# The front of an ordered list of steps rewritten: gate sums and tail before the first weights, first weight conversion before the first scores

## The chip, the cores and the metric

The kernel runs on one core of a Trainium2 chip. The metric is the device time of one execution in microseconds (us); the time before is the median of three runs. A core has five engines that each work through their own instructions in order and meet only through semaphores: TensorE (PE, matrix products; PEld is its weight load), VectorE (DVE), ScalarE (ACT), GpSimd (POOL) and SyncE (SP), which here issues nearly all transfers between device memory and the core.

## What is computed

An mLSTM-like recurrence over 32 sequences (4 batches, 8 heads, 768 steps, head size 40), whose output, laid out as 3072 tokens of 320 values, goes through a two-layer network with a piecewise quadratic between the layers:

```python
for t in range(S):
    m_new = np.maximum(f_gate[:, :, t] + m, i_gate[:, :, t])
    f_stab = np.exp(f_gate[:, :, t] + m - m_new)
    i_stab = np.exp(i_gate[:, :, t] - m_new)
    C = f_stab * C + i_stab * outer(v_t, k_t)
    n = f_stab * n + i_stab * k_t
    y[:, :, t] = sigmoid(o_gate_t) * (C @ q_t) / np.maximum(np.abs(n @ q_t), 1.0)
h = x @ w_in            # x: y as 3072 x 320, w_in 320 x 2048
g = np.where(h >= 1, h, np.where(h <= -1, 0, (h + 1) ** 2 / 4))
return g @ w_out        # w_out 2048 x 320
```

## The kernel before

The 768 steps are cut into 6 chunks of 128; chunk c of batch b is block n = 4c + b, so blocks 0 to 3 are the first chunks of the four batches. Four blocks give one tile of 512 tokens for the network (six tiles), each worked through in 16 slices of 128 hidden values.

The order of the work is a list written out by hand, `STEPS`: a string of names such as `main.0`, each of which runs one step of the program or the next part of a step that pauses (`main.0` stands in the list six times, once for each of its parts). A wrapper (`InOrder`) holds every engine to the order in which its instructions come from that list. The list orders each engine; how engines meet is settled by what they read and write, and by which of the eight PSUM banks (`ps`, 128 x 512 fp32) a product gets. All products take their bank from this one pool, and a bank is given again once its last reader is through.

Nearly every instruction carries the line number of the wrapper (L189) in the profile, so tiles tell the steps apart. The steps that the change and the prediction speak of:

- `fi`, `fb`, `id`, `cs`, `W.i`, `qk.n`, `vv`, `v.n`, `og`, `A.n`: transfers in, issued on SP. `id` brings `ident` (an identity matrix and constants). `W.0` brings `wraw`, the first eighth of w_in; `W.1` the first eighth of w_out. `qk.n` is two transfers into `raw` (queries and keys of block n), `vv` and `v` bring values (and keys) into `ow` or `vk`, `og.0` the output gates of chunk 0 into `sig`.
- `sums.0`, `gtail.0`: small VectorE instructions on the gates of chunk 0 (`fi`, `m`, `ah`, `ac`, `ex`), with copies on GpSimd. `gex.0`: TensorE transposes `ex`, ScalarE takes the exponentials into `G`.
- `mask.b` and `add.b`: two banks of exponents for block b; `mask` puts in the causal mask (`late_t`, `idb`), `add` sums of the gates (`pick`, `less`, `ac`). `dec.b.0` and `dec.b.1`: ScalarE takes the exponentials of the two banks into `Abc` (or `A` for block 3), and so frees them.
- `score.n`: products of queries and keys (`raw`) into two banks, then, in two more parts, VectorE multiplies `Abc` by them.
- `main.n`: the product of `Abc` with the scaled values (`v1.n` on GpSimd), the division, the gate `sig`, a transposition of the result `y` and its split into `xh` and `xl`, the input of the network.
- `bmax`, `bsum`, `btail`, `exps`: the gates of chunks 1 to 4 at once; in its second part `bmax.0` moves `m_r` to `m_b` by four transfers on SP.
- `w.0`: the five parts of the conversion of `W.0`: `mg` and `win` on ScalarE, `win` on VectorE, `wh` on ScalarE, `wl` on VectorE.
- `sig.0`: ScalarE's sigmoid over the gates of chunk 0. It is another table of functions than the exponentials', so an ACT_TABLE_LOAD stands ahead of it and another behind it.
- `hot.k`: k products of zeros with nobody reading them.
- `mm.x`, `relu.x`, `max.x`, `out.x`: the network's slices.

The lines that the prediction leans on most:

```python
nc.scalar.activation(sig[c], sig[c], AF.Sigmoid)                       # sig
...
nc.scalar.activation(A[:, 4 * hh:4 * hh + 4, :], T[n]["Ap"][hh]..., AF.Exp)   # dec, chunk 0
...
up = psum_a()                                                          # main, a bank
for h in range(H):
    nc.tensor.matmul(up[:, h * D1:(h + 1) * D1], M[:, h, :], t["v1"][:, h, :], start=True, stop=True)
```

Of the kernel before, what the change touches and what calls it, by code (L numbers as in the profile page):

```python
# [45 lines left out]


STEPS = (
    "fi.0 mask.1 fb.0 W.0 vv.0 mask.0 hot.2 sums.0 mask.3 qk.1 add.1 hot.2 add.0 qk.2 w.0 w.0 bmax.0 id.0 dec.1.0 "
    "dec.1.1 dec.0.0 score.1 qk.3 gtail.0 hot.2 hot.2 bmax.0 gex.0 score.1 mask.2 qk.0 add.2 dec.2.0 dec.2.1 vv.2 "  # L50
    "add.3 v.4 dec.3.1 v1.1 dec.3.0 score.1 og.0 W.1 dec.0.1 score.2 main.1 score.0 bsum.0 bsum.0 bsum.0 w.0 "
    "score.3 score.2 score.2 one.0 score.0 v.1 score.0 v1.2 btail.0 w.0 v1.0 sig.0 main.1 btail.0 hot.4 btail.0 "
    "btail.0 w.0 v1.3 main.0 score.3 v.0 main.0 W.2 hot.2 exps.0 main.0 main.1 main.2 hot.2 hot.2 qn.5 A.4 score.3 "
    "v2.4 main.2 main.2 main.0 w.1 v2.1 qk.4 main.0 w.1 cs.0 main.3 main.1 main.2 main.0 W.3 v.5 carry.4 main.3 "
    "main.3 hot.2 v2.0 qn.4 main.1 decs.0 main.1 v.2 w.1 carry.1 main.3 A.5 A.6 main.2 w.2 carry.0 main.2 main.3 "
    "main.3 prep.4 carry.0 w.2 v1.4 prep.4 v2.5 score.4 w.2 prep.4 decs.0 W.4 carry.1 w.3 -- score.4 mm.0 relu.0 "
    "max.0 mm.1 w.2 main.4 w.2 relu.1 main.4 W.5 carry.5 W.6 carry.4 v2.2 w.3 w.3 main.5 main.5 prep.5 prep.5 "
    "score.4 carry.2 carry.2 max.1 mm.3 relu.3 prep.5 mm.2 w.4 carry.5 qk.5 prep.6 main.4 relu.2 main.4 v1.5 max.3 "
    "w.4 w.4 carry.5 prep.6 w.5 qk.6 og.1 max.2 out.0 out.1 out.2 w.5 w.5 w.4 w.4 score.5 so.1 score.5 score.5 A.7 "
    "W.7 score.6 w.6 carry.4 carry.4 v.6 w.6 prep.7 score.6 prep.6 mm.5 w.6 score.6 v1.6 qn.6 sig.1 main.5 main.4 "  # L60
    "main.4 so.2 relu.5 so.2 max.5 main.5 mm.4 relu.4 w.6 main.5 w.6 qn.7 w.7 w.7 prep.7 out.3 main.6 main.6 main.6 "
    "v2.6 carry.6 max.4 mm.6 carry.5 w.7 gh.5 gl.5 carry.6 gh.4 so.3 so.3 v.3 v2.3 carry.3 W.8 outh.4.2.3 carry.6 "
    "w.8 w.8 mm.7 outh.4.0.1 gl.4 main.6 outl.4 outh.5.2.3 A.8 relu.6 carry.3 main.7 A.9 qk.7 score.7 w.8 main.5 "
# [965 lines left out]
```

## Time and profile before

| what | us |
|---|---|
| median of three runs (465.94, 466.06, 479.42) | 466.06 |
| the profiled execution's own time | 465.84 |
| its span, from the first to the last instruction | 464.1 |
| TensorE busy in it | 456.0 (98%) |
| VectorE, ScalarE, GpSimd busy | 350.7, 327.5, 144.1 |

The profile is of one execution. Times in its rows count from the start of the span; 1.74 us of the execution's own time lie around the span. Products are pipelined, so a busy TensorE says that it had products in flight, and the distance from one product's start to the next's says how fast they went.

### The profile page before, as it was taken

Reading aid. Unit: us, or ns where it says so; the run is one execution under the profiler, and the core shown is the slowest. Engines: PE = TensorE matmul, PEld = TensorE weight load, DVE = VectorE, ACT = ScalarE, POOL = GpSimd, SP = SyncE. Lnnn points to the kernel's source line nnn. Section 1 sums busy time; section 2 is a strip of 40 time slices with the busy share of each in tenths; the row PEclk is TensorE's granted clock in tenths of the full one; section 3 lists DMA queues with packets and bytes.
Section 4 is the critical chain, followed back from the end, with each engine's and each line's share of the span. In section 5 each row is a group of like instructions: output and inputs, shape, how many; then the busy total and the mean of one; then the engine's idle time right before and its main releaser. Section 6 shows DMA issues by size and latency. Waiting matters only on the chain.

```text
span 464.1 us, 8795 instructions
## 1 busy us (share of the span) xinstructions
PE 456.0 (98%) x3333; PEld 408.5 (88%) x3336; DVE 350.7 (76%) x625; ACT 327.5 (71%) x593; POOL 144.1 (31%) x153
## 2 busy tenths in 40 slices
PE   6999999999999999999999999999999999999996
PEld 3888789998899999999988899989988898989986
DVE  5786789998979889878999988786775985443523
ACT  3679999998985586877777666766777734464651
POOL 2364233212543624423425643433213231000000
PEclk9999999999999999999999999999999999999999
DMA  6899959726445442564165437234616000010001
GB/s 215 291 283 352 296 175 347 220 67 166 147 115 148 118 132 91 171 177 124 48 177 161 118 89 203 63 78 155 159 57 160 1 1 0 2 42 16 1 0 57
DMA packets 23048, 60.60 MB, mean 131 GB/s; under 512 B 2599, under 2 KB 9535, under 8 KB 23007
## 3 DMA queue, kind: packets, MB, share of 16 engines
q1 hardware_dynamic: 22719, 59.81, 43.2%
q8 instruction: 26, 0.43, 0.4%
q10 hardware_dynamic: 288, 0.25, 0.2%
q14 instruction: 15, 0.12, 0.1%
HBM read 55.96 MB, written 4.01 MB: 129 GB/s over the span
## 4 chain that ended last, share of the span: by engine, by line
PE 87%; DVE 4%; ACT 3%; DMA 3%; issue 1%; SPq 1%; DVEq 0%
PE ps L189 87%; DMA qs<-in_qs 1%; DMA ident<-in_cst 1%; ACT r L189 1%; DVE stk L189 1%; SPq L189 1%; DVE hv L189 1%; DVE r L189 1%; DVE gl L189 0%; ACT Abc L189 0%; ACT raw L189 0%; ACT win L189 0%; ACT mg L189 0%; DVE win L189 0%; DVE xl L189 0%
## 5 line engine op out<-in xcount | busy, mean ns | idle before, releaser
L189 PE MATMUL ps<-oh,gh 128*128 128x320 f32 x368 | 112.3, 315 | 0.1
L189 PE MATMUL ps<-ow,gh 128*128 128x320 f32 x368 | 110.1, 309 | 0.0
L189 PE MATMUL ps<-xh,wh 128*128 128x512 f32 x288 | 100.6, 403 | 0.1
L189 PE MATMUL ps<-xh,wl 128*128 128x512 f32 x288 | 98.2, 395 | 0.0
L189 ACT ACTIVATE r<-ps,half 128x512 f32<-128x512 f32 x96 | 65.6, 683 | 44.5 <-PE ps L189 39.4
L189 DVE SCALAR_TENSOR_TENSOR r<-ps,r 128x512 f32<-128x512 f32 x96 | 64.7, 685 | 39.0 <-ACT r L189 38.7
L189 DVE TENSOR_TENSOR gl<-r,gh 128x512 fp32r<-128x512 f32 x92 | 69.9, 769 | 25.7 <-ACT gh L189 24.7
L189 ACT CAST gh<-r 128x512 fp32r<-128x512 f32 x92 | 56.2, 617 | 46.4 <-PE ps L189 21.6
L189 PEld LDWEIGHTS ps<-oh,gh 128*128 128x128 f32 x368 | 69.1, 188 | 1.9 <-issue 0.3
L189 PEld LDWEIGHTS ps<-ow,gh 128*128 128x128 f32 x368 | 69.2, 188 | 1.3
L189 PE MATMUL ps<-oh,gl 128*128 128x320 f32 x368 | 70.2, 311 | 0.0
L189 PEld LDWEIGHTS ps<-xh,wl 128*128 128x128 f32 x288 | 54.1, 188 | 12.8
L189 ACT ACTIVATE r<-r 128x512 f32<-128x512 f32 x96 | 60.7, 633 | 3.0
L189 PE MATMUL ps<-xl,wh 128*128 128x512 f32 x192 | 60.3, 395 | 0.0
L189 PEld LDWEIGHTS ps<-oh,gl 128*128 128x128 f32 x368 | 58.1, 188 | 1.1
L189 PEld LDWEIGHTS ps<-xh,wh 128*128 128x128 f32 x288 | 50.3, 188 | 7.8 <-DVE Abc L189 0.2
L189 ACT ACTIVATE Abc<-Abc,nA 128x128 f32<-128x128 f32 x160 | 50.4, 391 | 0.1
L189 POOL TENSOR_TENSOR v<-vk,G 128x328 f32<-128x328 f32 x36 | 28.9, 807 | 53.2 <-DMA vk<-in_vk 28.2
L189 POOL TENSOR_TENSOR y<-y,z 128x320 f32<-128x320 f32 x24 | 21.1, 882 | 76.2 <-DVE y L189 76.2
L189 PEld LDWEIGHTS ps<-xl,wh 128*128 128x128 f32 x192 | 36.0, 188 | 8.8
L189 POOL TENSOR_TENSOR m<-m 128x1024 bf16<-128x1024 f32 x16 | 31.6, 1976 | 37.6 <-DVE m L189 35.0
L189 DVE SCALAR_TENSOR_TENSOR stk<-raw,ident,qs 120x1024 fp32r<-120x1024 f32 x28 | 37.9, 1356 | 2.9 <-ACT raw L189 2.8
(143 smaller groups left out, 665.4 us busy)
## 6 DMA issues: line engine op xcount, KB each, us to landing
qs<-in_qs SPq DMA_DIRECT2D x28, 480.0 KB
Abc<-a_d SPq DMA_DIRECT2D x20, 512.0 KB
vk<-in_vk SPq DMA_DIRECT2D x20, 324.0 KB
wraw<-in_w_in SPq DMA_DIRECT2D x8, 768.0 KB
wraw<-in_w_out SPq DMA_DIRECT2D x8, 640.0 KB
sig<-in_og SPq DMA_DIRECT2D x6, 640.0 KB
qn<-in_qn SPq DMA_DIRECT2D x20, 180.0 KB
raw<-in_qk SPq DMA_DIRECT2D x20, 160.0 KB
```

Source lines behind the costliest of these rows:

```text
L189: r = getattr(self.engine, name)(*args, **kwargs)
```

## The change

Only the string `STEPS` changes, and only its first 204 of 1621 words. The words are the same ones, each as often as before; from word 205 on (`mm.5`) the two lists are equal. The first lines of it:

```diff
-    "fi.0 mask.1 fb.0 W.0 vv.0 mask.0 hot.2 sums.0 mask.3 qk.1 add.1 hot.2 add.0 qk.2 w.0 w.0 bmax.0 id.0 dec.1.0 "
+    "fi.0 mask.1 fb.0 id.0 sums.0 gtail.0 W.0 mask.0 add.1 dec.1.0 dec.1.1 add.0 hot.2 hot.2 gex.0 w.0 w.0 bmax.0 "
```

What the list makes of each engine's order shows in the built programs. First SP's queue, the transfers behind the first three. Before (a number behind a name tells tiles of one name apart):

```order
L189 DMA wraw_139<-in_w_in 128x1536
L189 DMA ow_141<-in_vk 128x2x328
L189 DMA raw_174<-in_qk 40x2x512 x2
L189 DMA raw2_200<-in_qk 40x2x512 x2
L189 DMA ident_92<-in_cst 128x154
L189 DMA raw3_224<-in_qk 40x2x512 x2
L189 DMA m_b_239<-m_r_207 32x129 x4
L189 DMA raw_253<-in_qk 40x2x512 x2
L189 DMA ow_268<-in_vk 128x2x328
L189 DMA vk_280<-in_vk 128x648
L189 DMA sig_286<-in_og 128x1280
```

The same stretch of SP's queue with the changed list:

```order
L189 DMA ident_92<-in_cst 128x154
L189 DMA wraw_163<-in_w_in 128x1536
L189 DMA raw_231<-in_qk 40x2x512 x2
L189 DMA ow_234<-in_vk 128x2x328
L189 DMA raw2_251<-in_qk 40x2x512 x2
L189 DMA m_b_256<-m_r_205 32x129 x4
L189 DMA raw_265<-in_qk 40x2x512 x2
L189 DMA sig_279<-in_og 128x1280
L189 DMA ow_281<-in_vk 128x2x328
L189 DMA wraw_283<-in_w_out 128x1280
L189 DMA raw3_285<-in_qk 40x2x512 x2
```

`ident` is now ahead of the first weights, and the gates `sig` are ahead of the second pair of values (`ow`), of the values `vk` and of block 3's `raw3`.

Second, ScalarE from the first exponentials to the sigmoid. Here `Abc_143` is block 0 (banks 144 and 145), `Abc_130` block 1, `Abc_248` block 2 (banks 249 and 250), `A3` block 3. Before:

```order
L189 ACTIVATE Abc_143<-ps_144 128x512
L189 ACTIVATE G_117<-ps_244 128x128
L189 ACTIVATE Abc_248<-ps_249 128x512
L189 ACTIVATE Abc_248<-ps_250 128x512
L189 ACTIVATE A3_169<-ps_171 128x512
L189 ACTIVATE A3_169<-ps_170 128x512
L189 ACTIVATE Abc_143<-ps_145 128x512
L189 CAST wh_125<-win_205 128x3x256
L189 ACT_TABLE_LOAD
L189 ACTIVATE sig_286<-sig_286 128x1280
L189 ACT_TABLE_LOAD
```

ScalarE with the changed list, where `Abc_165` is block 0 and `Abc_226` block 2 (banks 227 and 228):

```order
L189 ACTIVATE win_203<-wraw_163 128x768
L189 ACTIVATE A3_210<-ps_212 128x512
L189 ACTIVATE A3_210<-ps_211 128x512
L189 CAST wh_125<-win_203 128x3x256
L189 ACTIVATE Abc_226<-ps_227 128x512
L189 ACTIVATE Abc_165<-ps_166 128x512
L189 ACTIVATE Abc_165<-ps_167 128x512
L189 ACT_TABLE_LOAD
L189 ACTIVATE sig_279<-sig_279 128x1280
L189 ACT_TABLE_LOAD
L189 ACTIVATE Abc_226<-ps_228 128x512
```

The last exponential of block 2 (`dec.2.1`, from bank 228) stood ahead of the sigmoid and now stands behind it and its two table loads.

Third, TensorE at `main.0`, behind its products of zeros, with what each row waits for. Before:

```order
L189 LDWEIGHTS zeros_90
L189 MATMUL ps_356<-zeros_90 128x512
L189 MATMUL ps_367<-ow_141,Abc_143 128x41 [waits DVE_49,Pool_49]
L189 MATMUL ps_367<-ow_141,Abc_143 128x41 x3
L189 MATMUL ps_367<-ow_141,Abc_143 128x41 [waits DVE_49]
L189 MATMUL ps_367<-ow_141,Abc_143 128x41 x3
```

The same place on TensorE with the changed list:

```order
L189 LDWEIGHTS zeros_90
L189 MATMUL ps_338<-zeros_90 128x512
L189 MATMUL ps_348<-ow_234,Abc_165 128x41 [waits DVE_49,Activation_49,Pool_49]
L189 MATMUL ps_348<-ow_234,Abc_165 128x41 x3
L189 MATMUL ps_348<-ow_234,Abc_165 128x41 [waits DVE_49]
L189 MATMUL ps_348<-ow_234,Abc_165 128x41 x3
```

The first product of `main.0` waited for VectorE and GpSimd and now waits for ScalarE too (Activation_49). In the built program it is a wait for ScalarE's thirteenth signal, which is given by `Abc_226<-ps_228`, the row behind the sigmoid; the bank of `main.0` (348) is the one that row reads.

## Rows read from the trace of the kernel before

**Rows 1.** The page's busy times: engine, busy us, share of the span, instructions.

```profile
PE 456.0 (98%) x3333; PEld 408.5 (88%) x3336; DVE 350.7 (76%) x625; ACT 327.5 (71%) x593; POOL 144.1 (31%) x153
```

**Rows 2.** The chain that ended last, in order of time: start, us, what.

```profile
12.07 7.82 PE ps L189 x88
...
302.27 158.24 PE ps L189 x1078
```

**Rows 3.** Busy us of each engine in two stretches; last, clock, DMA share, GB/s.

```profile
15.00:20.00 5.00, 4.95 (x63) 4.47 (x62) 4.76 (x12) 3.31 (x5) 2.61 (x3) 1.00 0.93 310
...
5.00:20.00 15.00, 13.17 (x132) 9.72 (x133) 10.30 (x26) 8.18 (x13) 4.86 (x8) 1.00 0.79 259
```

**Rows 4.** The timeline, TensorE to 7 us: start, us, engine, line, operation, tiles, count.

```profile
2.18 0.58 PE L186 MATMUL ps<-late_t,idb 128*128 128x512 bf16 x1 [2.18 <-POOL rst L186]
...
3.84 1.06 PE L189 MATMUL ps<-zeros 128*128 128x512 bf16 x2
...
5.59 0.39 PE L189 MATMUL ps<-ac,pick 96*128 96x128 bf16 x4
...
6.47 0.59 PE L189 MATMUL ps<-zeros 128*128 128x512 bf16 x2
...
6.91 0.39 PE L189 MATMUL ps<-ac,pick 96*128 96x128 bf16 x4
```

**Rows 5.** The timeline, TensorE from the gates' transposition to the third scores.

```profile
12.07 0.30 PE L189 MATMUL ps<-ident,ex 128*128 128x128 f32 x1 [0.23 <-DMA ident<-in_cst]
...
14.51 1.16 PE L189 MATMUL ps<-raw 40*128 40x128 f32 x16
...
15.60 1.98 PE L189 MATMUL ps<-ow,Abc 128*128 128x41 f32 x16
...
17.51 2.06 PE L189 MATMUL ps<-raw 40*128 40x128 f32 x32
```

**Rows 6.** The timeline, ScalarE; in brackets the idle time before, and its end.

```profile
6.95 0.90 ACT L186 ACTIVATE mg<-wraw 128x768 f32<-128x768 f32 x1 [4.93 <-DMA wraw<-in_w_in]
...
8.53 1.55 ACT L189 ACTIVATE Abc<-ps 128x512 f32<-128x512 f32 x3
...
14.62 1.09 ACT L189 ACTIVATE A<-ps 128x512 f32<-128x512 f32 x2 [0.24 <-PE ps L189]
...
17.43 0.83 ACT L189 CAST wh<-win 128x768 fp32r<-128x768 f32 x1 [1.25 <-DVE win L189]
...
21.25 1.27 ACT L189 ACTIVATE sig<-sig 128x1280 f32<-128x1280 f32 x1 [1.68 <-DMA sig<-in_og]
...
22.54 1.28 ACT L189 ACT_TABLE_LOAD   x1
...
23.83 0.66 ACT L189 ACTIVATE G<-ps 128x384 f32<-128x384 f32 x2
```

**Rows 7.** The timeline, VectorE: the scan of bmax.0, then gtail.0 and a copy.

```profile
6.68 1.27 DVE L189 TENSOR_TENSOR_SCAN m_r<-fi_r,m_r 32x512 f32<-32x512 f32 x1
...
7.99 0.28 DVE L189 TENSOR_TENSOR fi<-fi,m 32x128 f32<-32x128 f32 x1
...
9.19 0.14 DVE L189 COPY carry<-m_r 32x1 f32<-32x1 f32 x1
```

**Rows 8.** The timeline, SP's issues of m_b and of the gates sig.

```profile
7.98 3.37 SPq L189 DMA_DIRECT2D m_b<-m_r  x4
...
14.25 0.42 SPq L189 DMA_DIRECT2D sig<-in_og  x1
```

**Rows 9.** The transfers issued in the first 25 us: tiles, count, KB each.

```profile
raw<-in_qk SPq DMA_DIRECT2D x10, 160.0 KB
...
ow<-in_vk SPq DMA_DIRECT2D x2, 328.0 KB
...
vk<-in_vk SPq DMA_DIRECT2D x1, 324.0 KB
```

**Rows 10.** Busy us of each engine in the tail; then clock, DMA share, GB/s.

```profile
462.70:463.50 0.80, 0.00 (x0) 0.00 (x0) 0.00 (x0) 0.00 (x0) 0.00 (x0) 0.53 0.00 0
```

22 rows, old and new, of the table STEPS are left out of this document.

## The prediction

> **What bounds the kernel now.** I read the page's busy times first: TensorE is busy for 456.0 of 464.1 us [rows 1], so the span is TensorE's work plus some 8 us of waiting. The chain of waits says where those are: from 12.07 on it is TensorE's own products, with short detours, up to the last stretch, which ends at 302.27 + 158.24 = 460.51 [rows 2]. Then the stretches: between 15 and 20 us, in the middle of the part that is rewritten, TensorE is busy 4.95 of 5.00 us, while in the whole of 5 to 20 us it is busy 13.17 of 15 [rows 3]. So behind 12.07 nothing is waited for in the front, and what was waited before it, from 5 us on, is at most some 1.8 us. The list is a permutation: the products are the same, the products of zeros (`hot`) among them. Hence the rule for the sum: **the change costs or gives what it does to TensorE's idle time and to its rate in the front, and nothing else**. That ScalarE or VectorE do something earlier counts only where TensorE waits for it.
>
> **What the change removes.** The wait at 12.07 for `ident` [rows 5] goes: `ident` is fourth on SP's queue. Gate sums and tail run one behind the other on VectorE, ahead of the scan of `bmax.0`; that scan began at 6.68 and the tail took from 7.99 to 9.19, 1.20 us [rows 7]. So `ex` is ready 1.3 us earlier, and the scan and with it the `m_b` transfers, issued from 7.98 [rows 8], come 1.2 us later, at about 9.2. They stand ahead of `qk.0` and `og` on SP, so this holds back both; what they bring, `bsum` waits for, off TensorE's path until `exps`.
>
> **TensorE up to `main.0`.** Four mask products now run from 2.18 to some 3.9, where the products of zeros and `mask.3` followed before, and then TensorE waits for `ac` until 5.59 as it did [rows 4]. In the rows the products up to 3.84 start 0.42 us apart for 512 columns, which is 1.2 GHz, and at 6.47 two take 0.44, which is 2.4 GHz, though the clock column says 1.00 for all of it; TensorE had worked without a gap since 2.18 before the rate rose. With a gap of 1.7 us in that stretch the rise may come later. At the full rate `add.1` and `add.0` take 2 x 0.88 (5.59 to 6.47) and two pairs of zeros 2 x 0.44: the transposition of `ex` comes at 8.2. At half rate for as long as at the start (2.18 to 5.59, 3.4 us) 1.7 us are lost: 9.9. I take 9.9 and keep 8.2 for the range.
>
> From there to `main.0` TensorE has: transposition, one mask and two `add` 2.44 (12.07 to 14.51), `score.1`, `score.2`, `score.0` 1.09 each (14.51 to 15.60) [rows 5], another mask 0.44, and six pairs of zeros 2.62 [rows 4]: together 8.8. TensorE is ready for `main.0` at 17.0 to 18.7.
>
> **When `main.0` may start.** Its first product waits for `dec.2.1`, and that stands behind `sig.0` and two table loads. ScalarE, from the transposition at 9.9: `G` 0.34 later (12.07 to 12.41 is what it waited, and its row in the same stretch is 0.3 long), so free at about 10.5; `mg` and `win` 1.58 (6.95 to 8.53); two `A` 0.97; then `wh`, which waits for VectorE's `win` until about 13.1, 0.85; three `Abc` 1.45 to 1.55; one table load 1.28 [rows 6]: about 16.8. But `sig` also needs its gates. They landed at 21.25, where ScalarE had waited 1.68 us for them [rows 6], and were issued at 14.25 [rows 8]. With the new list 328 KB of `ow`, 324 KB of `vk` and 2 x 160 KB of `raw` (block 3) no longer stand ahead of them [rows 9]; at the 259 GB/s of 5 to 20 us [rows 3] these 972 KB are 3.75 us: 17.5. They can't be issued before about 12.1 to 13.2 (9.2, plus the four `m_b` in at most the 3.37 us of the row, plus `qk.0`), and 768 KB of `wraw`, nearly alone on the queues, took some 4.4 us from issue to `mg` at 6.95 [rows 6], so not before 16.0. I take 17.4, between 16.0 and 18.3.
>
> From the start of `sig` to the first work behind the second load the trace has 23.83 - 21.25 = 2.58; `dec.2.1` itself takes 0.6 [rows 6]. So `main.0` starts at 17.4 + 2.6 + 0.6 = **20.6**, and TensorE stands for 2 to 3.5 us.
>
> The Trainium skill, ScalarE: Activation LUTs, section What ACT_TABLE_LOAD costs, puts a switch at 2.66 us, 1.28 of load and 1.38 of drain. The load agrees with its row, but the next instruction starts at 23.83, 0.01 us behind the load [rows 6]: the trace shows no drain. By the page `main.0` would start 2.8 us later still; the row decides.
>
> **What that is worth.** Where would `main.0` have to start for the time to stay? Before, TensorE never waited from 12.07 on. Of the work that it did then, the new list has done ahead of `main.0`: 2.44 (transposition, mask, two `add`), two scores 2.18, and four of the pairs of zeros 1.75; the fifth score and the rest come behind it in both. Sum 6.4, less 0.1 for the two short gaps in these rows: 12.07 + 6.3 = **18.4** is break-even. So 20.6 - 18.4 = **+2.2 us**. Nothing behind can take it back, since TensorE did not wait there; nothing adds, if the order behind `main.0` keeps it fed: the `y` of `main.0` and `score.2` come through VectorE while TensorE has `main.1` (1.9 us, 15.60 to 17.51 [rows 5]) and a pair of zeros (0.44) to do, a cover of 2.3 us for the division on VectorE and one product on GpSimd. If that cover fails at one place, I allow 0.5, an estimate of one more VectorE instruction in the way. `w.0` done 4 us earlier is worth nothing: no product waited for it before, `mm.0` stands behind all four `main`.
>
> VectorE also does `wl` and two parts of `bsum` ahead of the products with `score.0`; `main.0` needs these products too. The wait for `dec.2.1` hides that; without it they would be next, and cost what they come after 18.7, when TensorE is ready.
>
> The sum is made against the profiled execution, 465.84, whose span is 464.1; it is 0.22 below the median. 465.84 + 2.2 = 468.0; on the median 466.06 + 2.2 = **468.3**.
>
> **The rivals.**
> 1. *The wait is as short as break-even, so not slower.* For this `sig` must begin by 18.4 - 3.2 = 15.2, so the gates must land within 3.1 us of the earliest issue and ScalarE be through its first load by then. The second can be, if the rate rises as early as before (16.8 less 1.7); the first has only the free queues for it, against 4.4 us of `wraw`. It would give 465.3 to 466.6. I give it 0.10; with what the change spares at 12.07 it reaches a gain of 0.5 at best.
> 2. *The clock falls while TensorE waits ahead of `main.0`, so slower still.* At the end of the trace TensorE's last product ended at 460.51 [rows 2], and from 462.70 to 463.50 the granted clock reads 0.53 [rows 10], about 1.2 GHz. So it had fallen some 2.2 us after the last product, and the wait that I expect is 2 to 3.5 us. From about 2.2 us on it decides: `main.0`, `main.1` and what follows run at half rate for a stretch like the one at the start, 3.4 us, and lose 1.7: 470.0. For it: the length. Against: one case, in the tail, where TensorE had nothing left. 0.25. The Trainium skill, TensorE: Matmul & The Clock Gate, section What's actually happening, also has the throttled clock as the idle state; no row here shows a wait of this length in the middle of the work.
>
> **The numbers.** Forecast 0.63, the clock 0.25, no slower 0.10, something else 0.02. The forecast's own bounds are the landing at 16.0 (where ScalarE's 16.8 takes over: `main.0` at 20.0, +1.6; with the early rise +1.2) and at 18.3 (+3.1, and 0.5 for a failed cover): 467.2 to 469.7. The range goes down to 466.5, which takes in a part of rival 1, and up to 470.7 for rival 2: outside is about 0.15. Two per cent, what a measurement tells from no change, are 9.3 us; no case comes near it, so faster 0.01, same 0.97, slower 0.02.
>
> **What would show it.** In the changed kernel's profile: `G` for chunk 0 near 10.3 and not 12.41; `wh` before 15 and not at 17.43; `sig` starting on a landing near 17.4; a wait of TensorE of 2 to 3.5 us that ends between 20 and 21.5 with ScalarE's `Abc` as its releaser, ahead of products from `ow` and `Abc`; no other wait of TensorE over 0.3 us behind it, and from `mm.5` on the same distances as before. I am wrong if that wait is under 1 us, if the gates land before 15.5, or if TensorE waits again further down for `xh`, `Abc` or weights.

## The result and the profile after

The changed kernel takes **470.48 us** (median of 4 executions, 470.39 to 470.60) against 466.09 for the kernel before on the same chip: a ratio of 1.0096, 95% interval 1.0079 to 1.0114. It is slower by 4.4 us where 2.2 were forecast. The profiled execution has a span of 468.7 us, 4.6 more than before. In some executions of several kernels here, the kernel before among them, the mean granted clock is only 0.97 to 0.98 and the time 473.5 us or more; the ratios leave most of those out, while the medians and ranges of single kernels include them.

The page's first lines of the changed kernel, span and busy time of each engine:

```profile
span 468.7 us, 8791 instructions
...
PE 459.4 (98%) x3333; PEld 410.4 (88%) x3336; DVE 352.1 (75%) x625; ACT 327.6 (70%) x593; POOL 142.4 (30%) x153
```

The same 3333 products are busy for 459.4 us, not 456.0 [rows 1]. So only 1.2 of the 4.6 us are idle time (9.3 instead of 8.1); **3.4 us are products that ran slower**. For that the forecast's sum had no term behind `main.0`.

TensorE's timeline, changed kernel (start us, us, what, count, in brackets the idle time ahead and what ended it):

```profile
5.65 0.58 PE L189 MATMUL ps<-ac,pick 96*128 96x128 bf16 x4 [1.60 <-DVE ac L189]
...
9.02 1.59 PE L189 MATMUL ps<-zeros 128*128 128x512 bf16 x4
10.44 0.27 PE L189 MATMUL ps<-ident,ex 128*128 128x128 f32 x1
...
15.58 1.90 PE L189 MATMUL ps<-zeros 128*128 128x512 bf16 x7
17.41 1.16 PE L189 MATMUL ps<-raw 40*128 40x128 f32 x16
18.50 1.04 PE L189 MATMUL ps<-zeros 128*128 128x512 bf16 x4
20.75 4.25 PE L189 MATMUL ps<-ow,Abc 128*128 128x41 f32 x32 [1.21 <-ACT Abc L189]
24.79 0.63 PE L189 MATMUL ps<-zeros 128*128 128x512 bf16 x1
25.64 0.42 PE L189 MATMUL ps<-ident,fi_b 128*128 128x128 f32 x1 [0.22 <-issue]
...
26.50 0.84 PE L189 MATMUL ps<-ident,y 128*128 128x128 f32 x3
...
28.36 0.55 PE L189 MATMUL ps<-ident,y 128*128 128x128 f32 x3
```

Read the same product in two places. Four products with `ac` lasted 0.39 at 5.59 before [rows 4]; at 5.65 they now last 0.58, and four zeros take from 9.02 to 10.44, 1.42 us, where two took 0.44 at 6.47 before [rows 4], so four 0.88. So TensorE is at 1.2 GHz up to some 10 us. Three transpositions of `y` last 0.84 at 26.50 and 0.55 at 28.36: it is at 1.2 GHz a second time. The windows of the changed kernel around that (last columns: granted clock, DMA share, GB/s) say from when to when:

```profile
20.75:23.80 3.05, 3.05 (x28) 3.05 (x28) 1.24 (x7) 0.00 (x0) 0.02 (x1) 1.00 1.06 307
23.80:27.21 3.41, 3.19 (x15) 2.66 (x15) 2.83 (x8) 0.47 (x2) 2.58 (x4) 0.50 0.98 348
27.21:30.00 2.79, 2.79 (x32) 2.61 (x32) 1.49 (x4) 2.67 (x8) 1.66 (x3) 1.00 1.00 350
```

From 23.80 to 27.21 the granted clock is 0.50. TensorE had 3.19 us of work there, half of which, 1.6 us, is the price. Of the rest of the 3.4, some 1.5 us belong to the first 10 us, which the forecast did see: TensorE worked about 6.3 us at the half rate there (2.19 to 4.05 and 5.65 to some 10.1), 3.4 before. Until it fell, TensorE had stood ahead of 20.75 and then run 28 of the 32 products of 128x41 in `main.0` and `main.1` without a gap.

ScalarE in the changed kernel, from `G` to the signal on which `main.0` waits:

```profile
10.75 0.28 ACT L189 ACTIVATE G<-ps 128x128 f32<-128x128 f32 x1 [2.60 <-PE ps L189]
...
13.69 0.83 ACT L189 CAST wh<-win 128x768 fp32r<-128x768 f32 x1
14.43 1.56 ACT L189 ACTIVATE Abc<-ps 128x512 f32<-128x512 f32 x3
16.01 1.28 ACT L189 ACT_TABLE_LOAD   x1
17.47 1.27 ACT L189 ACTIVATE sig<-sig 128x1280 f32<-128x1280 f32 x1 [0.17 <-DMA sig<-in_og]
18.75 1.28 ACT L189 ACT_TABLE_LOAD   x1
20.05 0.60 ACT L189 ACTIVATE Abc<-ps 128x512 f32<-128x512 f32 x1
```

From the landing of the gates on, this chain went as forecast, to within 0.15 us. The gates were issued at 12.74 and took 4.70 us (before 14.25 and 7.0).

### The profile page after: what moved, and what is told of

The parts are those of the page before. It is cut to its first block, busy times and chain, and to the rows that moved or that the text cites. A ratio compares the mean times of both kernels' runs of the same rounds, so it can differ in the third digit from the quotient of the medians.

```text
span 468.7 us, 8791 instructions
## 1 busy us (share of the span) xinstructions
PE 459.4 (98%) x3333; PEld 410.4 (88%) x3336; DVE 352.1 (75%) x625; ACT 327.6 (70%) x593; POOL 142.4 (30%) x153
## 4 chain that ended last, share of the span: by engine, by line
PE 95%; DMA 1%; DVE 1%; ACT 1%; SPq 1%; issue 0%; DVEq 0%
PE ps L189 95%; DMA sig<-in_og 1%; SPq L189 1%; DMA fi<-in_fi 0%; DVE m_r L189 0%; DVE fi L189 0%; ACT L189 0%; ACT sig L189 0%; DVE ac L189 0%; DVE ah L189 0%; DVE m L189 0%; ACT Abc L189 0%; ACT r L189 0%; DVE carry L189 0%; DVE less L186 0%
## 5 line engine op out<-in xcount | busy, mean ns | idle before, releaser
L189 DVE TENSOR_TENSOR gl<-r,gh 128x512 fp32r<-128x512 f32 x92 | 72.0, 791 | 25.3 <-ACT gh L189 24.3
```

The costliest lines, as they stand in the source:

```text
L189: r = getattr(self.engine, name)(*args, **kwargs)
```

## The experiments

Three theories were tried. **W** (in the first three expectations simply the theory): the standstill ahead of `main.0` lets the clock fall. **A** or **Z**: rows of thin products (`main`, 128x41) with no zeros among them do it, a standstill at most adding to them. **B**: the loss is only the half rate of the first 10 us. "The clock fell" below means a window at 0.50 behind the first rise; in an execution without one the mean clock reads 0.999 or 1.0, with one short stretch 0.996. By that measure it fell in the kernel before too, in 12 of 50 executions (in seven of them to 0.995 or 0.996, at 467.3 to 468.1 us). The diffs show only the words around each change of the list; the rest of a line is left out.

**1. `dec.2.1` ahead of `sig.0`** in the changed kernel.

```diff
-main.0 main.1 main.0 A.4 sig.0 main.0 hot.2 dec.2.1 btail.0
+main.0 main.1 main.0 A.4 dec.2.1 sig.0 main.0 hot.2 btail.0
```

> The changed kernel with dec.2.1 ahead of sig.0 in the list, so that the bank which main.0 takes over is read out before ScalarE turns to the gates; nothing else is moved. Theory (TensorE's wait for dec.2.1 puts main.0 at 20.75 instead of the break-even 18.4, and the half-rate stretch from 23.80 to 27.21 follows from that wait): main.0 starts near 19.4, where the last product of zeros ends and VectorE's score is done; no wait, the clock stays at 1.00; 470.5 - 1.4 - 1.7 = 467.4 us. Rival A (the clock falls because 32 thin products, 128x41, follow one another, wait or no wait): it falls some 3 us behind main.0's start, near 22.4; 470.5 - 1.4 = 469.1. Rival B (the loss is the half rate in the first 10 us, the wait only covers other waits): within 0.3 of 470.5.

468.28 us (467.68 to 471.47, 11 executions), ratio to before 1.0043 (1.0029 to 1.0057): half of the loss is gone. In eight of the eleven the clock read 0.999 or 1.0; in the profiled one, the longest, it fell twice, the first time although TensorE had not waited for anything since 5.5 us. Its timeline and windows:

```profile
18.00 1.04 PE L189 MATMUL ps<-zeros 128*128 128x512 bf16 x4
19.01 3.74 PE L189 MATMUL ps<-ow,Abc 128*128 128x41 f32 x32
22.57 0.39 PE L189 MATMUL ps<-zeros 128*128 128x512 bf16 x1
```

```profile
19.01:22.93 3.92, 3.92 (x34) 3.80 (x35) 3.31 (x12) 0.94 (x1) 0.89 (x2) 1.00 1.06 317
22.93:26.34 3.41, 3.29 (x22) 2.94 (x23) 1.94 (x6) 2.16 (x6) 3.09 (x5) 0.50 0.98 344
...
29.76:36.58 6.82, 6.60 (x32) 6.38 (x33) 3.49 (x12) 1.96 (x4) 4.93 (x6) 0.50 1.05 295
```

TensorE was busy for all of the 3.92 us ahead of the fall, so it need not stand for that; without the wait the fall is rarer, though (three of eleven; four of four in the changed kernel), and about as frequent as in the kernel before (12 of 50). The median lies between W (467.4) and A (469.1): the eight are nearer to W, while the profiled one shows that the fall does not need the wait. B is out.

**2. Zeros in the wait**, changed kernel.

```diff
-score.0 hot.4 A.6 btail.0 btail.0 main.0
+score.0 hot.10 A.6 btail.0 btail.0 main.0
```

> The changed kernel with hot.10 in place of hot.4 ahead of main.0: six products of zeros more, 6 x 0.217 = 1.3 us at the full rate, in the 1.4 us in which TensorE stood. They add work that the reference does not need. main.0 should start at 20.75 as in the changed kernel. Theory (the standstill lets the clock fall): the clock stays at 1.00 and the 1.7 us of the half-rate stretch go: 468.8. Rival A (the thin products make it fall): the stretch is still there, 470.5. Rival B (early half rate): 470.5 as well.

471.13 us (470.33 to 471.19, 4 executions). By its time this is A or B; its profile says otherwise:

```profile
19.56 2.33 PE L189 MATMUL ps<-zeros 128*128 128x512 bf16 x10
21.73 3.66 PE L189 MATMUL ps<-ow,Abc 128*128 128x41 f32 x32
```

```profile
21.73:25.66 3.93, 3.88 (x34) 3.74 (x34) 2.24 (x10) 0.00 (x0) 0.97 (x2) 1.00 1.03 306
25.66:32.87 7.21, 7.17 (x68) 6.69 (x68) 6.82 (x20) 3.15 (x8) 4.63 (x7) 1.00 0.87 310
32.87:36.28 3.41, 3.19 (x16) 3.24 (x16) 1.68 (x5) 2.09 (x5) 3.20 (x5) 0.50 1.05 287
```

With zeros right ahead, the same 32 products left the clock at 1.00. But `main.0` came 1 us later, since the clock's first rise came late in this execution and the zeros themselves had to be run, and the clock fell at 32.87, behind the next thin row (`main.2`, `main.3`). The expectation overlooked that row, and the gain at the first place was lost at the second. In all four executions the mean clock reads 0.996 or less, so here the clock fell each time with no wait ahead of the products.

**3. The wait kept, zeros between `main.0` and `main.1`**, changed kernel.

```diff
-main.0 main.1 main.0 A.4 sig.0 main.0 hot.2 dec.2.1
+main.0 hot.2 main.1 main.0 A.4 sig.0 main.0 dec.2.1
```

> The changed kernel with the pair of zeros hot.2, which follows main.1's products, put between those of main.0 and of main.1: the same products, the wait ahead of main.0 as it is, but the row of 32 thin products is cut into 16 and 16. Theory (the standstill decides): the clock falls near 23.8 as before, 470.5 within 0.4. Rival A (the long row of thin products decides): no fall, 468.8. Rival B: 470.5.

470.59 us (470.36 to 477.98): no change, as W said. In the profiled execution, the longest, the clock fell at 23.08, after a standstill of 1.63, `main.0` (20.73 to 22.51) and the two zeros. The other three read 0.996 as well. So 16 thin products behind a standstill are as bad as the 32.

**4. Zeros in the early gap**, changed kernel.

```diff
-W.0 mask.0 add.1
+W.0 mask.0 hot.4 add.1
```

> The changed kernel with hot.4 behind mask.0: four products of zeros more in the 1.6 us in which TensorE waits for ac near 4 us; they add work that the reference does not need. The clock should rise near 5.4 as in the kernel before, and the transposition of ex come at 8.7 instead of 10.44. Theory (the gates' landing at 17.4 and ScalarE behind it set main.0): main.0 still starts within 0.3 of 20.75, TensorE only waits some 3 us ahead of it; 470.2 to 471.5 with the fall of the clock. Rival B (the half rate of the first 10 us is what is lost): main.0 1.7 us earlier and 468.8.

478.78 us, the lowest 471.91: the time itself is not to be compared. Its profile answers the question, though:

```profile
9.31 0.27 PE L189 MATMUL ps<-ident,ex 128*128 128x128 f32 x1
...
17.37 1.04 PE L189 MATMUL ps<-zeros 128*128 128x512 bf16 x4
20.61 6.18 PE L189 MATMUL ps<-ow,Abc 128*128 128x41 f32 x32 [2.20 <-ACT Abc L189]
```

TensorE was 1.1 us earlier at `ex` and at the last zeros, and `main.0` stayed where it was: behind ScalarE. What the first 10 us lose is covered in the changed kernel, and B is out. In it TensorE stood 1 us longer, and the clock fell already at 21.53 and stayed down until 45.42; only one of the four executions came below 477 us.

**5. `dec.2.1` ahead of `sig.0`, and zeros moved into the early gap.**

```diff
-W.0 mask.0 add.1 dec.1.0 dec.1.1 add.0 hot.2 hot.2 gex.0
+W.0 mask.0 hot.2 hot.2 add.1 dec.1.0 dec.1.1 add.0 gex.0
```

> The run with dec.2.1 ahead of sig.0, and the two pairs of zeros that follow add.0 moved ahead of add.1, into TensorE's wait for ac: the same products as the changed kernel. Its measure is the run without this move, 468.28, and 467.7 in the executions whose clock did not fall. With zeros in that gap the clock rose at 7.88 instead of 9.28 to 10.14. Reason (early half rate and gap are paid as soon as ScalarE no longer sets main.0): ex is transposed near 8.5, main.0 starts 1.0 to 1.5 us earlier, near 17.5 to 18, no wait over 0.3 ahead of it; 466.2 to 466.9, so level with the kernel before (466.0). Rival (VectorE's score, behind wl and bsum, sets main.0 as well): it starts near 18.7 and no more than 0.3 us are gained: 467.5 or above. The thin products of main.0 and main.1 still stand in one row of 32, so that the clock may fall as in the run before, + 1.7 and more in such an execution.

467.70 us (465.78 to 471.78, 10 executions), ratio 1.0042 (1.0013 to 1.0071). `main.0` started at 17.97 in the profiled execution, 1.0 earlier than in experiment 1, and the shortest executions, 465.78, 466.08 and 466.34, are level with before, as expected: once ScalarE is out of the way, the early gap is paid. The median is higher, mainly because the clock fell in five of the ten (mean clock 0.989 to 0.996), in the profiled one at 27.20, in the products of `main.3`. Two executions whose clock did not fall took 467.18 and 468.09 all the same; why is not known, since they were not profiled.

**6. The same, with two pairs of zeros moved among the thin products.**

```diff
-v.1 score.2 hot.2 hot.2 v.0 bsum.0 cs.0 hot.2 dec.0.0
+v.1 score.2 hot.2 v.0 bsum.0 cs.0 dec.0.0
...
-main.0 main.1 main.0
+main.0 hot.2 main.1 main.0
...
-main.2 main.2 main.2 main.3 decs.0
+main.2 main.2 main.2 hot.2 main.3 decs.0
```

> The run before this one (dec.2.1 ahead of sig.0, zeros in the early gap) with two pairs of zeros taken out of the row of seven near 15 us and put between the products of main.0 and main.1 and between those of main.2 and main.3: no product more than in the changed kernel. Theory Z (the clock falls where thin products, 41 columns each, follow one another for long with no 512-column products among them, a standstill counting like them): no fall in the front in any execution, 466.3, and the executions within 1 us of one another. Theory W (the standstill decides): this run has none either, so no fall, and the run without the spread has none as well: the two within 0.3 of each other.

472.76 us (467.27 to 479.06, 9 executions), ratio 1.0104 (1.0059 to 1.0148): worse, and neither theory said so. The clock fell in seven of the nine. In the profiled execution, the longest, the place that the zeros were taken from suggests why:

```profile
13.12 1.04 PE L189 MATMUL ps<-zeros 128*128 128x512 bf16 x3
14.95 0.46 PE L189 MATMUL ps<-raw 40*128 40x128 f32 x2 [0.79 <-DMA raw<-in_qk]
15.87 1.13 PE L189 MATMUL ps<-raw 40*128 40x128 f32 x14 [0.47 <-DMA raw<-in_qk]
16.93 1.71 PE L189 MATMUL ps<-zeros 128*128 128x512 bf16 x4
18.44 3.48 PE L189 MATMUL ps<-ow,Abc 128*128 128x41 f32 x16
```

The row of seven had covered the first of these waits for `raw` (experiment 5 has only the second, 0.47). Now TensorE stood 0.79 and 0.47 us there, and the clock fell at 17.14, ahead of `main.0`, whose 16 products took 3.3 us instead of 1.7.

**7. The kernel before, its zeros moved out of the thin rows**, with no new wait for ScalarE.

```diff
-dec.0.1 score.2 main.1 score.0
+dec.0.1 score.2 hot.2 hot.2 hot.2 main.1 score.0
...
-main.0 W.2 hot.2 exps.0 main.0 main.1 main.2 hot.2 hot.2 qn.5
+main.0 W.2 exps.0 main.0 main.1 main.2 qn.5
```

> The kernel before the change, with three pairs of zeros (the one behind main.0's products, the two behind main.2's) moved ahead of main.1's products: the same products, no new wait for ScalarE, and none among the thin products from main.0 to the first zeros behind main.3, some 7 us. Theory Z (the row of thin products lets the clock fall): the granted clock falls to 0.5 between 22 and 30 us though TensorE never stands: 466.0 + 1.7 = 467.7, more if it stays low for longer. Theory W (only a standstill does it): clock 1.00, 466.0 within 0.5.

469.77 us (469.48 to 470.93), ratio 1.0090 (1.0075 to 1.0105), mean clock 0.989 to 0.992 in all four executions: Z, by the time. Timeline and windows:

```profile
21.43 1.88 PE L189 MATMUL ps<-ow,Abc 128*128 128x41 f32 x16
...
23.60 1.88 PE L189 MATMUL ps<-ow,Abc 128*128 128x41 f32 x16
26.20 0.90 PE L189 MATMUL ps<-ident,y 128*128 128x128 f32 x3 [0.73 <-POOL y L189]
26.90 3.48 PE L189 MATMUL ps<-ow,A 128*128 128x41 f32 x16
```

```profile
21.43:25.99 4.56, 4.05 (x37) 3.93 (x35) 4.35 (x16) 2.94 (x6) 0.56 (x1) 1.00 1.02 353
25.99:32.82 6.83, 6.62 (x32) 6.56 (x33) 4.19 (x14) 2.28 (x5) 4.04 (x7) 0.50 1.02 274
```

The stretch is twice as long as expected, 6.83 us, which costs 3.3; with the 0.73 us that TensorE now waits for `y`, 4.0, against the 3.7 measured. The fall came inside that short wait, so this run does not have thin products by themselves. It shows that these zeros must not be taken from their places, but not whether they hold the clock themselves or by covering the wait for `y`. Only the row at 19.50 of the kernel before is still in its place (20.55 here).

**8. The wait kept, but with zeros on both sides of it and among the thin products**, changed kernel.

```diff
-v.1 score.2 hot.2 hot.2 v.0 bsum.0 cs.0 hot.2 dec.0.0 hot.2 score.0
+v.1 score.2 hot.1 hot.1 v.0 bsum.0 cs.0 hot.1 dec.0.0 hot.1 score.0
...
-btail.0 btail.0 main.0 main.1 main.0
+btail.0 btail.0 hot.1 hot.1 hot.2 main.0 hot.2 main.1 main.0
...
-main.2 main.2 main.2 main.3 decs.0
+main.2 main.2 main.2 hot.2 main.3 decs.0
```

> The changed kernel with its wait for dec.2.1 as it is, but in front of a pair of zeros instead of main.0's products, and with a pair of zeros between main.0 and main.1 and one between main.2 and main.3; four products of zeros fewer in the row near 15 us, eight more behind it (they add work that the reference does not need). TensorE stands some 1.7 us up to 20.7, and no row of thin products is over 2 us long. Theory W (the standstill decides): the clock falls near 23.8 all the same: 466.0 + 2.35 + 3 x 0.43 for the pairs behind the wait + 1.7 = 471.4. Theory Z (the long row of thin products decides, the standstill only adds to it): clock 1.00 there, 469.7.

469.22, 469.27, 473.38 and 483.87 us, median 471.32: two executions with a clock of 1.0 and at the time that Z gave (469.7), two in which it fell; that the median is W's 471.4 is chance, no execution is near it. In the profiled one, 473.38, TensorE stood for 2.36 us up to 21.30, the zeros and `main.0` followed, and the clock fell at 23.50. So a standstill can let the clock fall even with zeros behind it. The two others should have had much the same wait, since nothing of ScalarE's work was moved, and came without a fall; they were not profiled. What decides in a single execution these runs do not tell.

**9. One part of the change alone, in the kernel before**: `ident` and the gates' tail early, `ex` and the sums of blocks 2 and 3 ahead of `score.1`, all from `main.1` on as it was.

```diff
-fi.0 mask.1 fb.0 W.0 vv.0 mask.0 hot.2 sums.0 mask.3 qk.1 add.1 hot.2 add.0 qk.2 w.0 w.0 bmax.0 id.0 dec.1.0
-dec.1.1 dec.0.0 score.1 qk.3 gtail.0 hot.2 hot.2 bmax.0 gex.0 score.1 mask.2 qk.0 add.2 dec.2.0 dec.2.1 vv.2
-add.3 v.4
+fi.0 mask.1 fb.0 id.0 W.0 vv.0 mask.0 hot.2 sums.0 gtail.0 mask.3 qk.1 add.1 hot.2 add.0 qk.2 dec.1.0 dec.1.1 gex.0
+add.3 w.0 w.0 bmax.0 mask.2 add.2 dec.0.0 score.1 qk.3 hot.2 hot.2 bmax.0 score.1 qk.0 dec.2.0 dec.2.1 vv.2
+v.4
```

> The kernel before the change with one part of the change alone: ident directly behind the first gates on SP, the tail of the gates behind their sums on VectorE, and on TensorE the transposition of ex, add.3, mask.2 and add.2 ahead of score.1, which waits 1.5 us for raw; ScalarE reads add.1 out (dec.1.0, dec.1.1) and makes G ahead of the first piece of w_in. Everything from main.1 on stays in the order of before, with its zeros between the thin products and dec.2.1 ahead of sig.0. If the loss lies where theory Z and the wait for dec.2.1 put it and not in the gates' move, this is no slower than before: TensorE has 2.3 us of work to do in its waits of 1.5 us for raw and 0.23 us for ident, 466.0 - 1.7 = 464.3 at best; the part comes back that other waits take (y behind the gates' landing, DMA of raw), so between 464.3 and 466.0. Rival (moving the gates ahead is itself what costs, by VectorE's scan 1.2 us later and its m_b): slower than 466.5.

465.74 us (464.84 to 474.85, 10 executions), ratio 0.9981 (0.9963 to 0.9999), five executions between 464.8 and 465.2. The gates' move costs nothing here; it gives about 1 us in half of the executions and makes the fastest kernel of this study. The clock fell in three of the ten.

```profile
10.99 1.16 PE L189 MATMUL ps<-raw 40*128 40x128 f32 x16
...
19.61 1.95 PE L189 MATMUL ps<-ow,Abc 128*128 128x41 f32 x16 [0.54 <-DVE Abc L189]
```

`ex` is transposed at 8.57, and the sums fill the wait for `raw`, which is gone at 10.99; part of it comes back as 0.54 for VectorE's score ahead of `main.0`.

**10. Experiment 5 with two pairs of zeros added among the thin products**, none taken away elsewhere.

```diff
-main.0 main.1 main.0
+main.0 hot.2 main.1 main.0
...
-main.2 main.2 main.2 main.3 decs.0
+main.2 main.2 main.2 hot.2 main.3 decs.0
```

> The run with dec.2.1 ahead of sig.0 and zeros in the early gap, and a pair of zeros more between main.0 and main.1 and between main.2 and main.3; this time none is taken out of the row near 15 us (they add work, 4 x 0.217 = 0.87 us, that the reference does not need). Theory Z (long rows of thin products and standstills let the clock fall): no fall, all executions within 1 us of each other, 466.1 + 0.9 = 467.0. If it still falls in some executions, as in the run with the zeros moved, where TensorE stood for 0.79 and 0.47 us behind a shorter row: the median is above 468 and the spread over 2 us, and zeros at these two places do not hold it.

466.63 us (466.21 to 468.21, 10 executions), ratio 1.0013 (0.9998 to 1.0028), with 0.87 us more work than experiment 5 and a median 1.1 us lower. Two executions still read 0.996, against five of ten with 0.996 or less there, and none is above 468.3. That is better than Z's 467.0, but Z's "no fall, within 1 us" is not met, and the intervals of the two ratios overlap (1.0013 to 1.0071 there): that the added zeros help is likely, not shown. The profiled execution, 468.21, had no fall; it waited 0.48 us for `raw` and 0.64 us for `qn`.

```profile
17.72 1.91 PE L189 MATMUL ps<-ow,Abc 128*128 128x41 f32 x16
19.46 0.60 PE L189 MATMUL ps<-zeros 128*128 128x512 bf16 x2
19.90 1.88 PE L189 MATMUL ps<-ow,Abc 128*128 128x41 f32 x16
```

Experiment 3 has the same zeros between `main.0` and `main.1` and the wait ahead of them, and there all four executions read 0.996 or less: that speaks for the wait's part.

## Why the prediction was half right

- **`ident`, `ex`, the early gap.** The wait at 12.07 went, TensorE waited for `ac` to 5.65, and the clock rose late: `ex` at 10.44 where 9.9 was taken. From there to the end of the zeros ahead of `main.0` it took 8.9 us (10.44 to some 19.4: 18.50 and 0.88), forecast 8.8. TensorE was ready 0.7 us later than the latest forecast, and so the sign "a wait of 2 to 3.5 us" was missed: the profile has 1.21. The start of `main.0` is not touched by that (experiment 4).
- **ScalarE.** `G` at 10.75 (forecast near 10.3), `wh` at 13.69, `sig` on the gates' landing at 17.47 (17.4), no drain behind the second load (20.05 against 18.75 + 1.28), `main.0` at 20.75 (20.6), released by `Abc`. Experiment 1 shows the cause: `dec.2.1` ahead of the sigmoid, and the wait is gone.
- **Break-even.** 20.75 - 18.4 = 2.35, forecast 2.2. One of the forecast's own bounds is off by its own terms: a landing at 16.0 with the early rise puts `main.0` at 19.2, which is +0.8 and not +1.2. The 18.4 is borne out: 465.84, plus the start of `main.0` less 18.4, plus half of TensorE's busy time at a clock of 0.50, gives the profiled executions of experiments 1 to 5 within 0.4 us (experiment 1: 465.84 + 0.61 + 4.95 = 471.40, measured 471.47; experiment 4: 465.84 + 2.21 + 11.73 = 479.78, measured 479.71).
- **The step that failed** is the sum behind `main.0`: "Nothing behind can take it back, since TensorE did not wait there; nothing adds, if the order behind `main.0` keeps it fed". TensorE was fed, no wait but one of 0.22 us followed, and 1.6 us were still added, because the same products ran at half rate from 23.80 to 27.21. 2.35 + 1.6 + 0.22 are 4.2 of the 4.6; the remaining 0.4 is not assigned. All of it is lost early: the products `xh`, `wh` at 57.16 before stand at 61.70 in the changed kernel.
- **Why it failed.** The sum put the rate of TensorE behind `main.0` at that of the kernel before without a reason, and took the products of zeros for plain work ("the products are the same, the products of zeros among them"). The kernel before has zeros between its thin rows (here the products of `main.0`, `main.2` and `main.3`):

```profile
19.50 1.04 PE L189 MATMUL ps<-zeros 128*128 128x512 bf16 x3
20.37 1.88 PE L189 MATMUL ps<-ow,Abc 128*128 128x41 f32 x16
22.07 0.60 PE L189 MATMUL ps<-zeros 128*128 128x512 bf16 x2
...
22.95 1.88 PE L189 MATMUL ps<-ow,Abc 128*128 128x41 f32 x16
24.66 1.03 PE L189 MATMUL ps<-zeros 128*128 128x512 bf16 x4
...
25.86 1.88 PE L189 MATMUL ps<-ow,A 128*128 128x41 f32 x16
```

The new list has twelve in two rows ahead of `main.0` (15.58 and 18.50; the trace has records of eleven) and then, up to the end of `main.3`, only the pair at 24.79. Experiment 7 takes the zeros out of the last two of those places of the kernel before and loses 3.7 us, though with a new wait of 0.73 us.

- **What let the clock fall is not settled.** For the wait: in the kernels whose profile shows TensorE waiting 0.73 to 2.20 us ahead of the products of `main.0` or among the thin rows (changed kernel, experiments 3, 4 and 7) the clock fell in all 16 executions, and once the wait for ScalarE is gone (experiment 1) about as often as in the kernel before. Against the wait alone: it fell in only two of four with 2.36 us and zeros on both sides (experiment 8), in all four of experiment 2, which fills the wait, and in experiment 1 once with no standstill ahead of it. That zeros among the thin rows hold the clock fits experiments 2, 7 and 10, but no run here shows it by itself.
- **Rival 2** had the right event and price (470.0, measured 470.48) at a chance of 0.25, but the wrong condition. It let the clock fall during the wait, from 2.2 us on; the wait was 1.21, and the fall came 3 us after it, in the thin products. The Trainium skill, TensorE: Matmul & The Clock Gate, section What's actually happening, ties the lower clock to an idle engine; the window 19.01 to 22.93 of experiment 1, busy from end to end by the profile, shows it behind a busy stretch.
- **Rival 1** (no slower) needed an earlier sigmoid; it landed as forecast and the rival fell.

## What to carry to other kernels

When the same products take longer in total, look at their rate before looking for waits: the busy sum (456.0 to 459.4) gave that away at once. A filler product has a place as well as a duration: when a list is reordered, check in every stretch of small products and short waits, the one that it is taken from too, which fillers are left. And when a bank is reused, whoever read it last can set the start of the next product: here a read of 0.6 us behind a sigmoid and two table loads.

## What was not expected of the hardware

- The clock fell in a stretch in which TensorE was busy all the time (19.01 to 22.93, experiment 1), and 3 us after a standstill rather than in it (20.75 and 23.80, changed kernel).
- Once down, it stayed down for 3.4 us in the changed kernel and experiment 2, 3.4 and then 6.8 in experiment 1, 6.8 in experiments 5, 7 and 8, and 20.5 to 27.3 in the profiled executions of experiments 3, 4 and 6 (23.08 to 43.56, 21.53 to 45.42, 17.14 to 44.45). In these last three it came back within 0.5 us of the first of the network's matrix products (43.82, 45.38, 44.90).
- The first rise moves from one execution to the next: with the same products up to there it came near 9.3 us in experiment 1, near 10.1 in the changed kernel and near 12.4 in experiment 2. At half rate in between, that is an estimate of up to 1.6 us by which the front of one kernel scatters.
